# Products of the identity ahead of the first scores, and the first loads in another order

## The chip, the core and the metric

The kernel runs on one core of one Trainium2 chip. The metric is the device time of one execution in microseconds, as the median of several runs. The engines are TensorE (PE in the profile; PEld is its loading of weights), VectorE (DVE), ScalarE (ACT), GpSimd (POOL) and SyncE (SP), whose queue issues all transfers between HBM and the core's memory.

## The reference

Attention over pooled keys and values feeds a gated layer. There are 8 batches, 8 heads, 576 positions, a head size of 64, and eight neighbouring keys (and values) are averaged to one, so that 72 remain:

```python
k_p = k.reshape(B, H, Sp, pool, D).mean(axis=3)
v_p = v.reshape(B, H, Sp, pool, D).mean(axis=3)
scores = scale * np.matmul(q, k_p.transpose(0, 1, 3, 2))
scores = scores - np.max(scores, axis=-1, keepdims=True)
attn = np.exp(scores)
attn = attn / (np.sum(attn, axis=-1, keepdims=True) + 1e-09)
x = np.matmul(attn, v_p)            # 4608 tokens x 512
a, b = x @ w_a, x @ w_b             # 512 x 1536 each
out = (a * b) @ w_out               # 1536 x 512
```

## The kernel before, in words

The 4608 tokens are 36 chunks of 128 tokens for the attention and 9 tiles of 512 tokens for the layer. The inner size 1536 is cut into 12 blocks f. Numbers of the layer are carried as a high and a low part (`xh`, `xl`; `jab` holds both parts of a block of `w_a` and `w_b`, `jo_open` those of `w_out`), and each product is three matmuls. Tiles 0 to 2 run one after the other (`psa`, `psb` are the two gates, `acc` the output); tiles 3 to 8 run in pairs with sums of blocks (`bank_psa`, `bank_psb`, `bank_att`, `pair`).

The opening is what the change touches. The first batch's keys come as four pieces `early_k` (they lie in the tile `wo_first`), each the rows of two heads. DVE sums eight neighbours (`kp`, L909), ACT scales the sums into a block-diagonal tile (`kdiag`, L914 to L916), and for each chunk of 128 queries TensorE makes the scores in two halves of four heads, `psc_..._0` from key pieces 0 and 1 and `psc_..._2` from pieces 2 and 3. DVE takes maxima (`m`), ACT exponentials (`s`), DVE the reciprocals (`z`) and the probabilities (`pr`, and a remainder `rem` for the last eight of the 72 pooled keys). TensorE turns those (`ptr`, `ptr_rem`), ACT copies them out (`early_p`, then `p`), and `po` is the product with the values, from which `xh` and `xl` follow. The first two batches' values and the second batch's keys are pooled by TensorE itself (`pvp` and `pkp`; a `pkp` matmul has only 16 columns). Four chunks (0 to 3) make tile 0; their queries are `early_q` (they lie in `wab_75` in the order of instructions).

Two things are made on the way: the identity `ident` (POOL), which the turning needs, and the weights, whose 64-bit words come over the same queue into `words_ab` and `words_o` and are turned into numbers by ACT and DVE (L528, L535, L251, L247).

The order of all instructions is not written out by hand. Every piece of work is a chain of operations with a rank (a due time), and `Schedule.run` places them one by one, on the engine whose next operation can start first by a table of costs (L175 to L200). Some operations may be placed on one of two engines: `pr` on DVE or POOL, `y` (the output's copy) on ACT or DVE. So an early edit can move operations much later. Each engine runs its own list strictly in that order. `load_early` (L486) is one chain with the highest rank; its transfers stand first in SP's queue. A chunk waits for the mark of its queries, and the loading of weight words for the mark of the last early queries (L506). Only the instructions at L1644 to L1646 are written ahead of the planner.

Of the kernel before, what the change touches and what calls it, by code (L numbers as in the profile page):

```python
# [19 lines left out]
P = 128  # L20
# [18 lines left out]
LAG = 5  # L39
BY_HEAD, LESS_MAX, COPIED = range(3)  # L40
PAIRED_OUT = 1, 2
PAIR_MARGIN, GIVE_MARGIN, SUMS_LATE = 0.0, 6.0, -30.0
XRANK, GIVE_ON, XON = -0.9, 0, ("dve", "pool")
LAGS = [2, 2, 2, 2, 4, 3]
# [36 lines left out]
class Schedule:  # L81
# [27 lines left out]
    def mark(self, *what):  # L109
        self.done.add(what)  # L110
# [93 lines left out]
def attn_moe_kernel(ctx: ExitStack, tc: tile.TileContext, q, k, kn, v, vn, vr, wa, wb, wo, out):  # L204
    nc = tc.nc
# [5 lines left out]
    mark, done = sch.mark, sch.done  # L211
# [10 lines left out]
    def place(pool, shape, dtype, tag, name):  # L222
        t = pool.tile(shape, dtype, tag=tag, name=name, bufs=1)
        sch.alias[t.name] = tag
        return t
# [47 lines left out]
    def dma(out, in_, rank=None):  # L273
        n = 4
        for d in out.shape:
            n *= d
        return Op((SD,), lambda e: nc.sync.dma_start(out, in_), [out], [in_], {SD: EVERY + n * BYTE}, rank)
# [36 lines left out]
    ident = const.tile([P, P], F32, name="ident")  # L314
# [6 lines left out]
    def xslot(x, name, dtype=F32R):  # L321
        return place(sb, [P, NK * NT], dtype, f"x{x}", name)
# [17 lines left out]
    early = sum(t == 0 for t in tile_of)  # L340
# [15 lines left out]
    jo = [xslot(6, "jo_open").rearrange("p (k h c) -> p k h c", k=2, h=2)]  # L356
    streamed = {("o", t1 * NF + f) for p, (_, t1) in enumerate(PAIRS) if p not in PAIRED_OUT for f in range(NF)}
    stream, combos, temps = {}, {}, []
# [6 lines left out]
    def bank(tag, name, dtype=F32):  # L365
        return place(ps, [P, 512], dtype, tag, name)
# [15 lines left out]
    early_q = wab[2][:, :early * 512].rearrange("p (c g s) -> p c g s", c=early, g=NK)  # L382
# [28 lines left out]
    for p, (t0, t1) in enumerate(PAIRS):  # L411
        order += [("both", p, f) for f in range(NF)] + [("rest", p, 0)]
        if p not in PAIRED_OUT:
            order += [("out", t1, f) for f in range(NF)]
    lasting = {"in": 24 * 0.228, "out": 12 * 0.228, "both": 54 * 0.228, "rest": 8 * 0.228}
    due, at = {}, 28.0
    for item in order:
# [3 lines left out]
        at += lasting[item[0]]  # L421
        if item[0] == "both" and item[1] in PAIRED_OUT:
            at += 9 * 0.228
# [4 lines left out]
    stored = {NF + f for f in range(LAG, NF)}  # L428
    apart = [pair for p, pair in enumerate(PAIRS) if p not in PAIRED_OUT]
    stored |= {t1 * NF + f for _, t1 in apart for f in range(NF)}  # L430
    uses, upcoming = [], {name: [] for name in ("ab", "o", "h")}
    for kind, t, f in order:
        if kind == "out":
            uses.append(t * NF + f)
        elif kind == "both" and t not in PAIRED_OUT:
            uses.append(PAIRS[t][0] * NF + f)
# [11 lines left out]
    def chunk_due(i):  # L448
        t = tile_of[i]
        if t < 2:  # L450
            return (-20.0 + 0.01 * i) if t == 0 else JOIN + STEP * (i - early)
        group = next((g for g in PAIRS if t in g), (t,))
        before = tile_due[group[0] - 1]
        share = (i * P + P - group[0] * NT) / (NT * len(group))
        return before + (tile_due[t] - before) * share - 45.0
# [3 lines left out]
    def queries(i):  # L459
        return q[i].rearrange("p (g s) -> p g s", g=NK)  # L460
# [3 lines left out]
    def rows_in(j):  # L464
        return min(P, S - j * P)
# [18 lines left out]
        mark("mask")  # L484

    def load_early():  # L486
        yield dma(early_q[:, 0], queries(0))
        mark("early_q", 0)
        for g in range(NK):
            yield dma(early_k[:, g, :], k[0, :, g, :])  # L490
            mark("early_k", g)
        yield dma(early_q[:, 1], queries(1))
        mark("early_q", 1)
        for j in range(NK + 1):
            rows = rows_in(j)
            yield dma(early_v[j][:rows], vn[0, j * P:j * P + rows])
            raws["v", 0, j] = early_v[j]
        for i in range(2, early):
            yield dma(early_q[:, i], queries(i))
            mark("early_q", i)  # L500

# [3 lines left out]
    def load_words(name):  # L505
        yield W(("early_q", early - 1))  # L506
        for f in range(NF):
            yield W(("converted", name, f - 1))
            for n, x in enumerate(name):
                yield dma(area[name][:, n * 1024:(n + 1) * 1024], w_dram[x][:, f, :].bitcast(I32), lead_of(name, f) - 6.0)  # L510
            mark("words", name, f)
# [144 lines left out]
    def loads():  # L656
# [4 lines left out]
        for p, (t0, t1) in enumerate(PAIRS):  # L661
            if p in PAIRED_OUT:
                for f in range(NF):
# [143 lines left out]
    def need(b):  # L807
        return min(chunk_due(i) for i in of_batch(b))

    def load_raw():  # L810
        yield W(("early_k", NK - 1))
        for kind, src in ("k", kn), ("v", vn):
            for j in range(NK + 1):
                n, rows = j + (NK + 1 if kind == "v" else 0), rows_in(j)
                if n < 8:
                    t = wab[1][:, n * DM:(n + 1) * DM]
                else:
                    kv_of[kind, 1, j] = yield from take(kv)
                    t = place(sb, [P, S], F32, kv_of[kind, 1, j], f"{kind}raw_1_{j}")
                yield dma(t[:rows, :DM], src[1, j * P:j * P + rows], need(1) - (20.0 if kind == "k" else 10.0))  # L820
                raws[kind, 1, j] = t
        for b in range(2, B):
            for kind in "kv":
                for x in range(NK if kind == "k" else NK + NG):
                    at = yield from take(kv)
                    t = place(sb, [P, S], F32, at, f"{kind}raw_{b}_{x}")
                    kv_of[kind, b, x] = at
                    if kind == "k":
                        yield dma(t, k[b, :, x, :], need(b) - 20.0)
                    else:  # L830
                        t = t[:, :D * POOL]
                        if x < NK:
                            yield dma(t, v[b, :, x, :], need(b) - 10.0)
                        else:
                            yield dma(t[:NR], vr[b, :, x - NK, :], need(b) - 10.0)
                    raws[kind, b, x] = t
# [805 lines left out]

    with tc.manual_schedule():
        nc.scalar.copy(rounded, ident)  # L1644
        for t in kdiag[0], unused, *vdiag, kdiag[1]:
            nc.gpsimd.memset(t.bitcast(F32), 0.0)  # L1646
        sch.free[SG], sch.free[SV] = 8.0, 2.0
        sch.spawn(load_early(), -5.0)
        sch.spawn(load_raw(), 0.0)
        sch.spawn(constants(), EIGHTH)  # L1650
        for b in range(B):
            sch.spawn(summed_keys(b) if b == 1 else load_keys(b), need(b) - 14.0 if b > 1 else need(b) - 3.0)
            sch.spawn(
                summed_values(b) if b < 2 else load_values(b),
                need(b) - 4.0 if b > 1 else need(b) - 1.0 if b else VALUES_0,
            )
        for i in range(NCH):
            sch.spawn(chunk(i), chunk_due(i))
        for name in ("ab", "o"):
            sch.spawn(load_words(name), 0.0)  # L1660
            sch.spawn(convert_weights(name), 0.0)
        for kind, t, f in order:
            if kind == "rest":
                continue
            x = (PAIRS[t][0] if kind == "both" else t) * NF + f
            if kind == "out":
                if t < 2:
                    sch.spawn(split_weight("o", x), due[kind, t, f] - 10.0)
                elif t < STD:
                    sch.spawn(load_weight("o", x), due[kind, t, f] - 8.0)  # L1670
                if x in stored:
                    sch.spawn(fetch_gated(x), due[kind, t, f] - 20.0)
            elif kind == "both":
                if t not in PAIRED_OUT:
                    sch.spawn(load_weight("o", x), due[kind, t, f])
            elif x < NF:
                sch.spawn(split_weight("ab", x), due[kind, t, f] - 8.0)
            elif not (t == 1 and f >= LAG):
                sch.spawn(load_weight("ab", x), due[kind, t, f] - 16.0)
        sch.spawn(sums_of_weights(), due["in", 1, NF - 1])  # L1680
        sch.spawn(loads(), 0.0)
        sch.spawn(attention_over(), 0.0)
        sch.spawn(sums_of_pairs(), 0.0)
        sch.spawn(late_places(), 0.0)
        for p in range(len(PAIRS)):
            sch.spawn(sums_of_x(p), due["both", p, 0] - 12.0)
        for t in range(2, STD):
            sch.spawn(whole_x(t), due["in", t, 0] - 15.0)
        sch.spawn(first_outs(), 1e9)
        sch.spawn(first_ins(), 2e9)  # L1690
        sch.spawn(main(), 2e9)
        sch.run()
# [51 lines left out]
```

## Time and profile before

| | |
|---|---|
| median of 3 runs | 978.2 us (976.83 to 978.72) |
| the profiled execution | 977.0 us, its span 975.2 us (the other 1.8 us lie around the span) |
| TensorE busy | 954.6 us, 98% of the span |
| DVE, ACT, POOL busy | 714.4, 414.4, 135.7 us |
| first matmul | 7.72 us after the span's start |
| mean granted clock of TensorE | 0.996 |

The page gives busy time by engine, then the span in slices. The chain that ended last is followed back from the last instruction: it names what the end waited for at every moment. A window's row gives, for a stretch of the span, the busy time of each engine with the number of instructions, then the granted clock of TensorE and the transfers. A row of the timeline is start, duration, engine, line, operation, out<-in, shape and count, and in brackets the idle time before it with what ended it. One fp32 matmul of the program is two records in the trace (the eight score matmuls of the first two chunks are 16 records), a transposition is one.

### The profile page before, as it was taken

Reading aid. Unit: us, or ns where it says so; the run is one execution under the profiler, and the core shown is the slowest. Engines: PE = TensorE matmul, PEld = TensorE weight load, DVE = VectorE, ACT = ScalarE, POOL = GpSimd, SP = SyncE. Lnnn points to the kernel's source line nnn. Section 1 sums busy time; section 2 is a strip of 40 time slices with the busy share of each in tenths; the row PEclk is TensorE's granted clock in tenths of the full one; section 3 lists DMA queues with packets and bytes.
Section 4 is the critical chain, followed back from the end, with each engine's and each line's share of the span. In section 5 each row is a group of like instructions: output and inputs, shape, how many; then the busy total and the mean of one; then the engine's idle time right before and its main releaser. Section 6 shows DMA issues by size and latency. Waiting matters only on the chain.

```text
span 975.2 us, 13044 instructions
## 1 busy us (share of the span) xinstructions
PE 954.6 (98%) x4502; PEld 788.6 (81%) x4502; DVE 714.4 (73%) x1182; ACT 414.4 (42%) x849; POOL 135.7 (14%) x113
## 2 busy tenths in 40 slices
PE   6999999999999999999999999999999999999997
PEld 5778888888888888888888878878888787888885
DVE  6899889899575864789845448156668989676687
ACT  5897656565554553554331124134221422412230
POOL 1001000000000000111212222122212425212221
PEclk9899999999999999999999999999999999999999
DMA  9789899899888999589888899776555756875632
GB/s 311 249 295 316 282 321 319 282 332 327 295 301 288 316 327 294 185 295 312 286 254 272 253 344 341 240 267 215 170 171 173 264 176 197 265 218 169 198 118 87
DMA packets 134978, 251.75 MB, mean 258 GB/s; under 512 B 10688, under 2 KB 46784, under 8 KB 134912
## 3 DMA queue, kind: packets, MB, share of 16 engines
q1 hardware_dynamic: 134912, 250.91, 76.9%
q8 instruction: 36, 0.59, 0.3%
q14 instruction: 30, 0.25, 0.1%
HBM read 191.37 MB, written 59.51 MB: 257 GB/s over the span
## 4 chain that ended last, share of the span: by engine, by line
PE 90%; DVE 4%; DMA 3%; ACT 2%; issue 0%; SPq 0%; POOL 0%; DVEq 0%; ACTq 0%; POOLq 0%
PE acc L303 16%; PE bank_psb L303 13%; PE psa L303 10%; PE psb L303 10%; PE bank_att L303 10%; PE bank_psa L303 9%; PE pair L303 8%; PE psc L303 4%; PE po L303 4%; PE last_acc L303 2%; PE ptr L300 2%; PE last L303 1%; DMA pair_tmp<-od 1%; PE pvp L303 1%; DMA words_ab<-in_wb 1%; DMA j<-jd 1%
## 5 line engine op out<-in xcount | busy, mean ns | idle before, releaser
L303 PE MATMUL bank_psb<-x,j 128*128 128x512 f32 x648 | 166.2, 391 | 1.0 <-DVE x L240 0.4
L303 PEld LDWEIGHTS bank_psb<-x,j 128*128 128x128 f32 x648 | 120.8, 188 | 27.7 <-DVE x L240 0.9
L303 PE MATMUL bank_psa<-x,j 128*128 128x512 f32 x432 | 110.8, 392 | 1.3 <-ACT pr L262 1.3
L303 PE MATMUL bank_att<-x,j 128*128 128x512 f32 x432 | 110.7, 391 | 0.7 <-DVE late_p L240 0.5
L303 PE MATMUL psb<-xh,jab 128*128 128x512 f32 x288 | 101.0, 400 | 0.0
L303 PE MATMUL psa<-xh,jab 128*128 128x512 f32 x288 | 99.3, 397 | 0.6 <-DVE jab L240 0.5
L303 PEld LDWEIGHTS bank_att<-x,j 128*128 128x128 f32 x432 | 80.4, 188 | 18.6 <-DVE late_p L240 0.9
L303 PEld LDWEIGHTS bank_psa<-x,j 128*128 128x128 f32 x432 | 80.4, 188 | 18.5 <-ACT pr L262 1.7
L303 PEld LDWEIGHTS psa<-xh,jab 128*128 128x128 f32 x288 | 53.9, 188 | 12.3 <-DVE jab L240 1.2
L303 PEld LDWEIGHTS psb<-xh,jab 128*128 128x128 f32 x288 | 54.1, 188 | 10.7
L303 PE MATMUL acc<-jo_later,hh 128*128 128x512 f32 x192 | 62.2, 405 | 0.1
L303 PE MATMUL acc<-jo_open,hh 128*128 128x512 f32 x192 | 61.4, 401 | 0.0
L303 PE MATMUL psa<-xl,jab 128*128 128x512 f32 x144 | 56.3, 391 | 0.0
L303 PE MATMUL psb<-xl,jab 128*128 128x512 f32 x144 | 56.2, 390 | 0.0
L240 POOL TENSOR_TENSOR x<-x,x 128x512 fp32r<-128x512 f32 x7 | 11.2, 1611 | 289.3 <-ACT x L262 287.4
L303 PEld LDWEIGHTS psc<-kdiag,q 128*128 128x128 f32 x288 | 42.4, 191 | 5.8 <-issue 1.2
L303 PE MATMUL psc<-kdiag,q 128*128 128x144 f32 x288 | 46.8, 290 | 0.1
L303 PE MATMUL po<-p,vdiag 128*128 128x256 f32 (+3 forms) x184 | 44.4, 345 | 0.5 <-ACT p L262 0.5
L303 PE MATMUL pair<-combos_jo,w 128*128 128x512 f32 x153 | 40.1, 393 | 1.7 <-DVE sums_tmp L240 0.9
L303 PEld LDWEIGHTS acc<-jo_open,hh 128*128 128x128 f32 x192 | 34.5, 188 | 6.1
L303 PEld LDWEIGHTS acc<-jo_later,hh 128*128 128x128 f32 x192 | 33.6, 188 | 5.6 <-ACT hh L262 0.5
L303 PE MATMUL acc<-jo_later,hl 128*128 128x512 f32 x96 | 37.9, 395 | 0.1
(287 smaller groups left out, 1914.3 us busy)
## 6 DMA issues: line engine op xcount, KB each, us to landing
j<-jd SPq DMA_DIRECT2D x108, 512.0 KB, 6.6
jab<-jd SPq DMA_DIRECT2D x34, 512.0 KB, 6.0
jd<-jab SPq DMA_DIRECT2D x24, 512.0 KB, 4.9
jo_later<-od SPq DMA_DIRECT2D x24, 512.0 KB, 5.1
w<-wd SPq DMA_DIRECT2D x44, 256.0 KB, 5.2
j<-jd SPq DMA_DIRECT2D x36, 256.0 KB, 6.9
w<-od SPq DMA_DIRECT2D x33, 256.0 KB, 5.0
q<-in_q SPq DMA_DIRECT2D x32, 256.0 KB, 5.7
```

The costliest lines, as they stand in the source:

```text
L240: run = lambda e: vec[e].tensor_tensor(out=out, in0=in0, in1=in1, op=op)
L300: nc.tensor.transpose(to, lhs, rhs)
L303: nc.tensor.matmul(to, lhs, rhs, start=start, stop=stop, skip_group_check=bool(skip))
```

## The change

First, twenty fp32 products of the 128x128 identity with itself are issued on TensorE ahead of everything that the planner places. They go to the bank `acc0`, which the first scores also use, and nobody reads them. Second, `load_early` loads the first two key pieces ahead of the first queries, and the queries of chunks 1 to 3 ahead of the first batch's values; before, the first queries came first of all, and those of chunks 2 and 3 after the values.

```diff
+QUERIES_AT, BEFORE_V, WARM = 2, 4, 20
...
     def load_early():
-        yield dma(early_q[:, 0], queries(0))
-        mark("early_q", 0)
         for g in range(NK):
+            if g == QUERIES_AT:
+                yield dma(early_q[:, 0], queries(0))
+                mark("early_q", 0)
             yield dma(early_k[:, g, :], k[0, :, g, :])
             mark("early_k", g)
-        yield dma(early_q[:, 1], queries(1))
-        mark("early_q", 1)
+        for i in range(1, BEFORE_V):
+            yield dma(early_q[:, i], queries(i))
+            mark("early_q", i)
         for j in range(NK + 1):
             rows = rows_in(j)
             yield dma(early_v[j][:rows], vn[0, j * P:j * P + rows])
             raws["v", 0, j] = early_v[j]
-        for i in range(2, early):
+        for i in range(BEFORE_V, early):
             yield dma(early_q[:, i], queries(i))
             mark("early_q", i)
...
         nc.scalar.copy(rounded, ident)
+        for n in range(WARM):
+            warm = bank("acc0", "warm") if not n else warm
+            nc.tensor.matmul(warm[:, :P], ident, ident, start=True, stop=True)
```

The head of SP's queue, before (`wab_75` with `in_q` are queries, `wo_first` key pieces, `wo_rest` and `wab_75` with `in_vn` values, `words_ab` weight words):

```order
L277 DMA wab_75<-in_q 128x512
L277 DMA wo_first<-in_k 128x576 x4
L277 DMA wab_75<-in_q 128x512
L277 DMA wo_rest<-in_vn 128x512 x4
L277 DMA wab_75<-in_vn 64x512
L277 DMA wab_75<-in_q 128x512 x2
L277 DMA words_ab<-in_wa 128x1024
L277 DMA words_ab<-in_wb 128x1024
```

and with the change:

```order
L278 DMA wo_first<-in_k 128x576 x2
L278 DMA wab_75<-in_q 128x512
L278 DMA wo_first<-in_k 128x576 x2
L278 DMA wab_75<-in_q 128x512 x3
L278 DMA wo_rest<-in_vn 128x512 x4
L278 DMA wab_75<-in_vn 64x512
L278 DMA words_ab<-in_wa 128x1024
L278 DMA words_ab<-in_wb 128x1024
```

The same thirteen transfers stand ahead of the weight words; the first queries went behind two key pieces, and two loads of queries went ahead of five of values.

The head of TensorE's list, before (`psc` scores, `pvp` pooled values, `ptr` turned probabilities; the last number of a name tells the tile's instance):

```order
L303 MATMUL psc_0_161<-kdiag_77,wab_75 128x144 x2
L303 MATMUL psc_0_167<-kdiag_77,wab_75 128x144 x2
L303 MATMUL psc_2_174<-kdiag_77,wab_75 128x144 x2
L303 MATMUL psc_2_175<-kdiag_77,wab_75 128x144 x2
L303 MATMUL pvp_0_199<-wo_rest,wab_75 128x512 x3
L303 MATMUL psc_0_218<-kdiag_77,wab_75 128x144 x2
L303 MATMUL pvp_0_199<-wo_rest,wab_75 128x512
L303 MATMUL psc_2_222<-kdiag_77,wab_75 128x144 x2
L300 MATMUL ptr_237<-ident,pr_216 128x128 x4
```

and with the change:

```order
L1650 MATMUL warm<-ident 128x128 x20
L304 MATMUL psc_0_180<-kdiag_77,wab_75 128x144 x2
L304 MATMUL psc_0_188<-kdiag_77,wab_75 128x144 x2
L304 MATMUL psc_2_195<-kdiag_77,wab_75 128x144 x2
L304 MATMUL psc_2_196<-kdiag_77,wab_75 128x144 x2
L304 MATMUL psc_0_204<-kdiag_77,wab_75 128x144 x2
L304 MATMUL psc_2_217<-kdiag_77,wab_75 128x144 x2
L304 MATMUL pvp_0_223<-wo_rest,wab_75 128x512 x4
L301 MATMUL ptr_263<-ident,pr_244 128x128 x4
```

The warm products stand in front, and the scores of the third chunk moved ahead of all pooled values.

TensorE's list between the last `po` of the first 256 tokens and the first `po` of the next 256, before (`pkp` the second batch's keys, `ptr_rem` the turned remainder):

```order
L303 MATMUL pkp_226<-eighth,wab_74 128x16 x4
L303 MATMUL pkp_226<-eighth,wab_74 128x8 x4
L300 MATMUL ptr_371<-ident,pr_342 128x128 x4
L300 MATMUL ptr_rem<-rounded,rem_343 96x128 x2
L300 MATMUL ptr_393<-ident,pr_324 128x128 x4
L300 MATMUL ptr_rem<-rounded,rem_325 96x128 x2
L303 MATMUL psc_0_407<-kdiag_77,q_187 128x144 x2
L303 MATMUL po_0_413<-p_1_366,vdiag_79 128x256
```

and with the change:

```order
L304 MATMUL pkp_253<-eighth,wab_74 128x16 x2
L301 MATMUL ptr_371<-ident,pr_338 128x128 x4
L304 MATMUL pkp_253<-eighth,wab_74 128x16 x2
L301 MATMUL ptr_rem<-rounded,rem_339 96x128 x2
L304 MATMUL pkp_253<-eighth,wab_74 128x16
L304 MATMUL pkp_253<-eighth,wab_74 128x8 x4
L301 MATMUL ptr_412<-ident,pr_383 128x128 x4
L301 MATMUL ptr_rem<-rounded,rem_384 96x128 x2
L304 MATMUL po_0_428<-p_1_369,vdiag_79 128x256
```

The third chunk's probabilities are turned between the small `pkp` matmuls instead of after them, and the scores ahead of `po` now follow it. After that the lists differ in many places (TensorE up to row 1425 of some 1920, DVE up to row 714 of 1143), and in which engine takes an operation: with the change POOL has three of the `pr` (before none), one `xl` (before none) and one more low part of the sums `x`, and one less of `jo_open`; DVE has three of the twenty copies `y` that ACT had. From there to the end all lists agree.

## Prediction

> **What bounds the kernel now.** I read the page's busy times first, then the span in stretches of 25 us, then the chain of waits over the first 75 us, and last the granted clock.
>
> ```profile
> PE 954.6 (98%) x4502; PEld 788.6 (81%) x4502; DVE 714.4 (73%) x1182; ACT 414.4 (42%) x849; POOL 135.7 (14%) x113
> 0.00:25.00 25.00, 17.28 (x100) 14.62 (x100) 16.72 (x37) 14.24 (x54) 4.68 (x19) 1.00 0.96 310
> 25.00:50.00 25.00, 24.58 (x121) 19.67 (x121) 22.00 (x38) 21.28 (x50) 0.00 (x0) 0.86 0.75 254
> 50.00:75.00 25.00, 23.45 (x124) 18.86 (x123) 23.51 (x48) 22.88 (x74) 0.00 (x0) 1.00 0.85 294
> 75.00:100.00 25.00, 25.00 (x119) 20.69 (x118) 22.64 (x33) 17.25 (x31) 2.64 (x2) 1.00 0.89 314
> 375.00:400.00 25.00, 25.00 (x126) 20.96 (x126) 14.00 (x28) 10.16 (x22) 0.00 (x0) 1.00 0.86 263
> ```
>
> After the length of each stretch come the busy times of PE, PEld, DVE, ACT and POOL, then the clock. From 75 to 400 us TensorE is busy without a gap, and from 400 us on the change leaves every list as it was. So what TensorE gains in the first 75 us it keeps to the end, if the new order opens no gap between 75 and 400 us; and it can gain nothing there. In the first 75 us there are three losses: 7.7 us before the first matmul, a clock of 0.86 between 25 and 50 us, and 1.55 us of gaps between 50 and 75 us, where ACT and DVE are over 90% busy. The chain shows them one by one:
>
> ```profile
> 1.66 4.50 DMA wo_first<-in_k
> 7.72 4.18 PE psc L303 x16
> 11.90 2.92 PE pvp L303 x6
> 14.82 0.49 PE psc L303 x4
> 15.31 0.86 PE pvp L303 x2
> 16.17 0.49 PE psc L303 x4
> 23.67 1.20 PE po L303 x6
> 24.87 2.15 PE pkp L303 x16
> 27.03 1.06 PE ptr L300 x4
> 28.11 0.85 ACT p L262 x2
> 30.02 1.08 PE psc L303 x4
> 31.10 3.36 PE po L303 x12
> 39.85 1.39 PE psa L303 x6
> 65.47 0.94 ACT jab L262
> 66.44 1.24 DVE jab L240
> ```
>
> Sixteen score records take 4.18 us at first, 0.26 each, and four take 0.49 us at 14.82, 0.12 each: TensorE starts slow and is at full rate about 4.6 us after its first matmul, although the records grant it 1.00 there. The weight loads date the change:
>
> ```profile
> 7.69 3.86 PEld L303 LDWEIGHTS psc<-kdiag,wab 128*128 128x128 f32 x16 [7.69 <-issue]
> 11.46 0.58 PEld L303 LDWEIGHTS pvp<-wo_rest,wab 128*128 128x128 f32 x2
> 12.52 0.19 PEld L303 LDWEIGHTS pvp<-wo_rest,wab 128*128 128x128 f32 x1 [0.48 <-issue]
> 12.95 0.19 PEld L303 LDWEIGHTS pvp<-wo_rest,wab 128*128 128x128 f32 x1 [0.24 <-issue]
> 26.00:26.50 0.50, 0.50 (x5) 0.50 (x5) 0.50 (x3) 0.50 (x3) 0.00 (x0) 0.62 0.41 143
> 32.50:33.00 0.50, 0.50 (x4) 0.41 (x2) 0.50 (x1) 0.07 (x1) 0.00 (x0) 0.55 1.01 418
> ```
>
> From 12.52 us on a load for `pvp` follows every 0.43 us; from 11.46 to 12.52 there are two, at 0.53. The rise lies near 12.3 us, 4.6 us after the first matmul. Later the clock falls again. A mean of 0.62 in the half microsecond from 26.0 and of 0.55 in that from 32.5 puts the slow stretch at 26.12 to 32.95, 6.83 us. It follows the long run of `pkp` (16 columns) and `ptr`, with no dense matmul between the `po` that ends at 24.87 and the scores at 30.02.
>
> [...]
>
> **The start, step by step.** The warm products need only `ident`:
>
> ```profile
> 1.49 0.30 POOL masks.py:199 TENSOR_SCALAR_AFFINE_SELECT ident<-ident 128x128 f32<-128x128 f32 x1
> 8.47 0.66 ACT L915 ACTIVATE kdiag<-kp 64x144 f32<-64x144 f32 x2 [0.84 <-DVE kp L255]
> 16.66 0.44 PE ptr L300 x4
> ```
>
> They start at about 1.85 us. Twenty are 40 records. A record costs 0.24 us slow (3.86 over 16; the slow `ptr`, also 128 columns, took 1.06 over 4, so 0.27) and 0.12 at full rate (0.49 over 4; `ptr` at full rate 0.44 over 4, so 0.11). If the rise comes 4.6 us after the start again, 19 records are slow and 21 fast: 1.85 + 4.6 + 2.5 = 9.0 us. The bounds of the rise are 3.4 and 6.8 us (half and all of the slow stretch), which gives 8.4 and 10.1 us. The first scores stand behind the products on TensorE's queue. Their keys and queries cannot need longer than before (7.72), so the warm products delay them by 0.7 to 2.4 us against before: the earlier keys are hidden completely behind them. Being issued first, those pieces only make sure that `kdiag` waits ready.
>
> From 9.0 us all runs at full rate: six groups of scores (three chunks) at 0.49 and four pairs of `pvp` at 0.86 are 2.94 + 3.44 = 6.4 us, so 15.4 us. The second half of the scores needs the fourth key piece, which is still the fifth transfer of the queue; its `kdiag` stands at 8.47 + 0.66 = 9.1, before the first two groups are through (10.0). Before, the same work ended at 16.17 + 0.49 = 16.66 us. TensorE leads by **1.3 us** (bounds 0.2 and 1.9, from 10.1 and 8.4 us).
>
> **The transfers.** Two loads of queries pass five of values.
>
> ```profile
> 3.55 1.86 SPq L277 DMA_DIRECT2D wo_rest<-in_vn  x4
> 6.18 0.57 SPq L277 DMA_DIRECT2D wab<-in_vn  x1
> 6.93 1.07 SPq L277 DMA_DIRECT2D wab<-in_q  x2
> wab<-in_vn SPq DMA_DIRECT2D x1, 128.0 KB, 6.3
> 14.66 0.65 PE L303 MATMUL psc<-kdiag,wab 128*128 128x144 f32 x4
> ```
>
> At 310 GB/s (the first stretch's rate), 512 KB are 1.7 us. The last values, issued at 6.18 before (6.3 us to landing, 12.5), land by about 14; the last `pvp` of the run of four wants the fourth piece at 11.9 + 3 x 0.86 = 14.5, the fifth piece only later. Cost nothing, hidden behind the scores of three chunks; without them it would be about 1 us. The third chunk's queries, which before landed near 13 and were used at 14.66, are now there when the second chunk's scores end. Weight words stand where they stood: no change.
>
> **The light stretch.** The lead of 1.3 us reaches the `pkp` and `ptr` work. With the change that work is interleaved, but there is still no dense matmul from the `po` of the first 256 tokens (before, end 24.87) to the next, and that one waits for ACT:
>
> ```profile
> 26.12:32.95 6.83, 6.41 (x27) 5.36 (x26) 5.98 (x12) 5.46 (x13) 0.00 (x0) 0.50 0.45 154
> 16.00:26.00 10.00, 10.00 (x81) 9.43 (x79) 8.02 (x23) 8.70 (x32) 0.00 (x0) 1.00 1.04 320
> 60.00:68.00 8.00, 6.45 (x35) 4.65 (x34) 7.37 (x15) 7.87 (x27) 0.00 (x0) 1.00 0.87 277
> ```
>
> So I expect the clock to fall again for about as long. Whatever of the lead lies within the slow stretch is worth half. Of the 6.83 us before, the chain lies 1.9 us (28.11 to 30.02) nearly all with ACT and DVE; the other 4.9 us are TensorE's work at half rate, so 2.5 us were lost. [...]
>
> **From 40 to 75 us** ACT is busy 7.87 of 8 us: the chain goes through ACT `jab` and DVE `jab`, which feed the next gates. ACT and DVE have the same work as before, so they pass the lead on: 0.9, and the gaps of 1.55 us stay (bounds: gone, or double).
>
> **From 75 to 400 us** the order is new, with three `pr` and one `xl` on POOL.
>
> ```profile
> L240 POOL TENSOR_TENSOR x<-x,x 128x512 fp32r<-128x512 f32 x7 | 11.2, 1611 | 289.3 <-ACT x L262 287.4
> L240 DVE TENSOR_TENSOR pr<-s,z 128x512 f32<-128x512 f32 x20 | 13.8, 690 | 0.6
> ```
>
> An operation of this size takes 1.61 us on POOL and 0.69 on DVE, 0.92 more, four times 3.7 us. They are hidden behind the gates' matmuls (1.4 us for six), as everything was there before; I take nothing, with 0 and 3.7 as bounds.
>
> **Sum.** 1.3 - 0.4 = 0.9 us faster. Against the profiled execution that is 977.0 - 0.9 = 976.1; it was 1.2 under the median, so the forecast against the median is 978.2 - 0.9 = **977.3 us**. Since a measurement of this kernel tells about 0.2% (2.0 us) from no change, this reads as the same.
>
> **Rivals.**
>
> *The clock does not fall.* The `pkp` run is now cut by `ptr` and `ptr_rem`. If that counts as activity, 2.5 us come back: 978.2 - 1.3 - 2.5 = 974.4. For it: before, the clock stayed 1.00 from 16 to 26 us in a mixture of scores, `pkp`, `ptr` and `po`. Against it: scores and `po` are missing from the new stretch. Chance 0.15.
>
> [...]
>
> *The lead is eaten.* [...] The same. Chance 0.17.
>
> *The opening gaps go.* With everything earlier, the 1.55 us between 60 and 68 us vanish too: 978.2 - 0.9 - 1.55 = 975.8. Against it: ACT is full there. Chance 0.05.
>
> *Slower: a POOL `pr` holds TensorE.* Where DVE has a turn to spare, a `pr` on POOL ends 0.92 us later, and `ptr` stands in TensorE's fixed list between dense matmuls, so a late `pr` stops all of them. From more than the margin that the planner left (over 2.9 us in all) it decides: four on the path are 978.2 - 0.9 + 3.7 = 981.0. Against it: between 75 and 400 us nothing waited before. Chance 0.13.
>
> The forecast itself (lead of 0.3 to 1.9, so 976.3 to 977.9) has 0.50. Faster: 0.15 + 0.05 and 0.10 of the forecast's upper end, 0.30; slower 0.13; the same 0.57. The range that leaves out two in ten is 974.8 to 980.0.
>
> **What would show it.** Right: `warm` of 40 records from 1.9 to about 9.0 us; the following `psc` at 0.12 us a record; `ptr` of the first chunk near 15.4; a granted clock of 0.50 again between about 25 and 33 us; TensorE busy 25.00 in each stretch from 75 to 400 us. Wrong: no stretch at 0.50 (a gain near 3.8 us), or a first `psc` after 10 us, or a gap that names `pr` on POOL as its releaser.

## The result and the profile after

The changed kernel takes 983.15 us (median of six runs, 982.59 to 987.2) against 976.63 us for the kernel before measured beside it (974.74 to 978.72). The ratio, which is that of the means, is 1.0077 with a 95% interval of 1.0061 to 1.0093: **slower by 7.5 us between the means and 6.5 us between the medians**, where 0.9 us faster was forecast, and outside the range. Three executions that lie far above all others, two of the kernel before (near 1946 us) and one of a kernel of the experiments (1372 us), are left out of every median and ratio here. The profiled execution took 982.64 us, its span is 980.9 us, 5.7 more than the 975.2 of before.

The opening went better than forecast. TensorE's rows of the timeline of the changed kernel, in its first 16 us (start, duration, engine, line, operation, shape and count):

```profile
1.84 6.40 PE L1650 MATMUL warm<-ident 128*128 128x128 f32 x40 [1.84 <-POOL ident masks.py:199]
8.35 3.18 PE L304 MATMUL psc<-kdiag,wab 128*128 128x144 f32 x24
11.36 3.60 PE L304 MATMUL pvp<-wo_rest,wab 128*128 128x512 f32 x8
14.79 0.60 PE L301 MATMUL ptr<-ident,pr 128*128 128x128 f32 x4
```

The first `ptr` stands at 14.79 (forecast 15.4; before, in the same view, 16.50). The first gate product `psa` starts at 34.58 us, before at 39.59; 0.5 us of that is a group of scores that stood ahead of it before and now follows.

Then TensorE loses more than it won. The stretches of 25 us in which the changed kernel's TensorE is idle (length, then busy time of PE, PEld, DVE, ACT, POOL, clock, transfers):

```profile
0.00:25.00 25.00, 23.06 (x155) 20.41 (x155) 18.21 (x43) 17.19 (x60) 4.67 (x19) 1.00 0.96 315
25.00:50.00 25.00, 23.50 (x117) 17.86 (x117) 21.42 (x35) 20.81 (x48) 0.00 (x0) 1.00 0.85 294
50.00:75.00 25.00, 20.96 (x106) 17.22 (x105) 21.72 (x45) 19.87 (x68) 0.00 (x0) 0.93 0.79 270
200.00:225.00 25.00, 24.19 (x118) 20.00 (x117) 21.77 (x39) 15.13 (x27) 1.29 (x1) 1.00 0.93 313
375.00:400.00 25.00, 24.24 (x127) 20.14 (x125) 14.60 (x26) 10.54 (x24) 0.00 (x0) 1.00 0.80 262
400.00:425.00 25.00, 23.17 (x132) 19.68 (x132) 20.45 (x38) 16.09 (x34) 2.70 (x2) 1.00 0.46 149
550.00:575.00 25.00, 23.69 (x105) 19.29 (x104) 9.71 (x15) 4.89 (x9) 5.14 (x4) 1.00 0.92 286
```

and those of before that the prediction did not show:

```profile
200.00:225.00 25.00, 25.00 (x123) 20.95 (x122) 23.06 (x42) 15.21 (x29) 0.00 (x0) 1.00 0.94 334
400.00:425.00 25.00, 24.86 (x133) 20.73 (x132) 20.04 (x37) 15.52 (x33) 4.38 (x3) 1.00 0.66 220
550.00:575.00 25.00, 24.82 (x110) 20.20 (x109) 8.30 (x12) 3.59 (x6) 5.18 (x4) 1.00 0.92 313
```

More idle than before, stretch by stretch: 1.1 (25 to 50), 2.5 (50 to 75), 0.8 (200 to 225), 0.8 (375 to 400), 1.7 (400 to 425) and 1.1 us (550 to 575), together 8.0. In the first 25 us idle time and warm products come to 0.6 more than the idle time of before. Against these 8.6 us stands work done in less time: TensorE is busy 958.1 us, of which 6.4 are the warm products, so 951.7 for all the rest, 2.9 less than the 954.6 of before (at the start the 24 score records take 3.18 us, 0.13 each, and the clock is 1.00 instead of 0.86 between 25 and 50 us). 8.6 - 2.9 = 5.7 us, the difference of the spans.

The waits of TensorE in the changed kernel (who waited, for whom: us in all, times, longest):

```profile
PE psc L304 <- ACT p L263: 2.3, 2, 1.7
PE warm L1650 <- POOL ident masks.py:199: 1.8, 1, 1.8
PE acc L304 <- DVE hl L241: 1.8, 1, 1.8
...
PE acc L304 <- ACT s L271: 1.7, 1, 1.7
PE bank_att L304 <- ACT temp L263: 1.3, 1, 1.3
PE psc L304 <- ACT s L263: 1.3, 2, 0.8
```

From 40 to 80 us, the kernel before has only these:

```profile
PE psa L303 <- DVE jab L240: 0.5, 1, 0.5
PE po L303 <- ACT p L262: 0.5, 1, 0.5
PE ptr_rem L300 <- ACT s L270: 0.5, 1, 0.5
```

No row of the change names POOL, apart from the start, where the products wait for `ident`. What such a wait is, ACT and then TensorE show at 52 to 55 us:

```profile
52.06 1.04 ACT L263 CAST jab<-wab 128x1024 fp32r<-128x1024 f32 x1 [1.88 <-DVE wab L241]
53.01 0.61 ACT L263 CAST hh<-h 128x512 fp32r<-128x512 f32 x1
53.53 0.58 ACT L263 COPY p<-ptr 128x512 f32<-128x512 f32 x1
...
51.91 0.60 PE L301 MATMUL ptr<-ident,pr 128*128 128x128 f32 x4
54.16 0.76 PE L304 MATMUL psc<-kdiag,q 128*128 128x144 f32 x4 [1.65 <-ACT p L263]
```

The turned probabilities `ptr` were there at 52.5, and the next scores need the bank that their copy `p` frees. But ACT's list has two casts ahead of the copy, the first of which waited for DVE until 52.06 itself. So the copy came at 53.53, and TensorE, whose list is as fixed, stood for 1.65 us. At 65 us four exponentials hold a bank that `acc` wants (1.67 us). In the stretch from 550 us a copy of `bank_att` comes late on ACT behind two casts (1.3 us). There ACT's order is that of before, and it is DVE that makes the sums for the casts later than before (the first cast waits 1.47 us for them).

This is one execution of the changed kernel. Three more traces of the same lists are in the next section (the changed kernel again, the loads alone, and the lists without either edit). Five rows of the list of waits stand in all four: `psc` behind `p`, `acc` behind `s`, `acc` behind `hl`, `bank_att` behind `temp` and `po` behind `p`. Together they are 8.1 to 8.5 us, where the two traces of the kernel before have 2.1 and 2.9 us of waits in all between 10 and 600 us. The idle time from 200 to 225 and from 375 to 400 us does not recur so: the other three traces have 0.4, 0 and 0 us there.

### The profile page after: what moved, and what is told of

Same layout as the page of the kernel before. It is cut to its first block, busy times and chain, and to the rows that moved or that the text cites. A ratio compares the mean times of both kernels' runs of the same rounds, so it can differ in the third digit from the quotient of the medians.

```text
span 980.9 us, 13141 instructions
## 1 busy us (share of the span) xinstructions
PE 958.1 (98%) x4542; PEld 791.8 (81%) x4542; DVE 715.6 (73%) x1181; ACT 413.7 (42%) x846; POOL 140.1 (14%) x117
## 5 line engine op out<-in xcount | busy, mean ns | idle before, releaser
L304 PE MATMUL pair<-combos_x,w 128*128 128x512 f32 x144 | 37.0, 390 | 0.7 <-DVE sums_tmp L241 0.7
```

The lines of the kernel that those rows point to most:

```text
L304: nc.tensor.matmul(to, lhs, rhs, start=start, stop=stop, skip_group_check=bool(skip))
```

## Experiments

The change does two things at once. Its edits (products, loads) act on the chip directly. And since the planner gets other loads, it makes other lists for every engine. The rivals were: the loads or the products themselves cost; the re-made list costs, whatever the edits do; and, for the second group, whether it is this list in particular (because the planner knows nothing of the products, or of how the new loads land) or any list that is made anew, that of before being a good draw. The letters D (a draw) and S (something special to this change) in the expectations of that group mean these two. Ratios are to the kernel before measured beside each kernel; for the three groups measured together it took 975.87, 976.08 and 975.94 us.

**The products alone.** The kernel before with the twenty products; the lists and loads are those of before.

```diff
         nc.scalar.copy(rounded, ident)
+        for n in range(20):
+            warm = bank("acc0", "warm") if not n else warm
+            nc.tensor.matmul(warm[:, :P], ident, ident, start=True, stop=True)
```

> The twenty products alone; transfers and every engine's list as before. Theory L (the list that the planner made anew costs the time): no slower than before; the first scores start near 8.4 us as in the changed kernel but at full rate, so 974 to 976.5 us, and TensorE has no gap between 75 and 400 us. Rival W (the products cost the time, by holding TensorE's queue or by what they do to its clock later): 980 to 983 us.

Measured: 976.77 us, ratio 1.0006 (0.9993 to 1.0019), just above the range of theory L and far from that of W. The products neither cost nor bring anything that can be told from nothing. One gap stands between 75 and 400 us against the expectation, 1.3 us for a load of queries; the second trace of the kernel before has it too (0.8 us).

**The loads alone**, with the lists that the planner makes of them.

```diff
-QUERIES_AT, BEFORE_V, WARM = 2, 4, 20
+QUERIES_AT, BEFORE_V, WARM = 2, 4, 0
```

> The two edits of the loads alone, with the list that the planner makes of them (that of the change, without the products). Theory L: 983 to 986 us, with the gaps of the changed kernel between 200 and 225, 375 and 425 and 550 and 575 us. Rival W: 976 to 977 us.

Measured: 983.76 us, 1.0085 (1.0063 to 1.0108). The whole loss is here, without a single warm product. Of the expected gaps those from 400 to 425 (1.8 us) and from 550 to 575 us (1.4) are there, those from 200 to 225 and from 375 to 400 us are not.

**Both edits on the chip, the lists of before.** The planner is shown the loads of before, and each of the thirteen transfers that it places issues the one that the change has at that place. TensorE, DVE, ACT and POOL keep their lists of before word for word.

```diff
+        for planned, real in zip(early_loads(0, 2), early_loads(2, 4)):
+            op = dma(*early_load(*planned))
+            op.run = lambda e, real=real: nc.sync.dma_start(*early_load(*real))
+            yield op
```

> Both edits carried out on the chip (twenty products, transfers in the new order), but the planner is told the old order of loads, so that PE, DVE, ACT and POOL keep the list of before word for word, and SP's differs only in its first thirteen transfers. Theory L: 973 to 976 us, faster than before. Rival T (the order of transfers costs the time, values coming late): 980 to 983 us.

Measured: 976.15 us, 1.0004 (0.9993 to 1.0016): no loss, but not the gain that theory L expected either.

**Neither edit on the chip, the lists of the change.** The same the other way round: no products, transfers in the order of before, the planner shown the new one.

```diff
+        for planned, real in zip(early_loads(2, 4), early_loads(0, 2)):
```

> The opposite: no products, the thirteen transfers in the old order, but the planner is told the new order, so that PE, DVE, ACT and POOL have the list of the change. Theory L: 982 to 986 us, the loss of the change without its edits. Rivals W and T: 976 to 978 us.

Measured: 984.06 us, 1.0095 (1.0064 to 1.0126). The waits from 10 to 600 us are those of the change:

```profile
PE psc L303 <- ACT p L262: 2.3, 2, 1.7
PE acc L303 <- DVE hl L240: 1.8, 1, 1.8
PE acc L303 <- ACT s L270: 1.7, 1, 1.7
PE bank_att L303 <- ACT temp L262: 1.4, 1, 1.4
```

These two runs settle the main question. The edits without the list cost nothing that can be measured, the list without the edits costs everything.

**Other lists, made without either edit.** In the planner's table the time that a transfer takes to land is raised by 10 ns, and in a second kernel the fixed part of a transfer's time by 1 ns.

```diff
-BYTE, EVERY, LAND, AHEAD = 1 / 330e3, 0.1, 1.8, 1.5
+BYTE, EVERY, LAND, AHEAD = 1 / 330e3, 0.1, 1.81, 1.5
...
+BYTE, EVERY, LAND, AHEAD = 1 / 330e3, 0.101, 1.8, 1.5
```

> Neither edit. The planner's table alone is touched: it believes that a transfer lands after 1.81 instead of 1.80 us. That has no meaning on the chip, but the lists differ from TensorE's row 30 on, in about as many places as those of the change. Theory S (the list of the change is slow because of what it was told, queries ahead of values): 975 to 977 us, as before. Theory D (any list that is made anew is a draw, and the list of before is a good one): anywhere from 976 to 986 us, slower than before in most cases, with gaps of TensorE at other places than in the changed kernel.

Measured: 987.61 us, 1.0126 (1.0103 to 1.015), slower than even theory D allowed.

> Neither edit. The planner believes that each transfer costs 0.101 instead of 0.100 us beside its bytes. Theory S: 975 to 977 us. Theory D: another draw, 976 to 986 us, not the time of the run with 1.81 us.

Measured: 981.53 us, 1.0061 (1.0046 to 1.0076). Of the 4210 rows of TensorE's list at least 515 would have to be moved to make the order of before into that of the change, 503 and 554 for these two. Their waits, of the first and then the second, from 10 to 600 us:

```profile
PE bank_att L303 <- ACT temp L262: 2.7, 1, 2.7
PE po L303 <- ACT p L262: 1.2, 1, 1.2
PE psa L303 <- DVE jab L240: 1.0, 1, 1.0
PE psc L303 <- ACT p L262: 0.9, 1, 0.9
```

```profile
PE bank_att L303 <- ACT temp L262: 1.4, 1, 1.4
PE po L303 <- ACT p L262: 1.2, 1, 1.2
PE psa L303 <- DVE jab L240: 1.0, 1, 1.0
PE psc L303 <- ACT p L262: 0.9, 1, 0.9
```

The kind is the same (TensorE behind a copy or a cast on ACT or DVE), mostly at other tiles. Theory S, which expected no loss from either, is out. A change of 10 ns in a table, with no work altered, costs at least as much as the whole change under study, and one of 1 ns nearly as much.

**The planner told of the products.** The products, the loads of before, and TensorE taken until 9.0 us in the planner's book.

```diff
         sch.free[SG], sch.free[SV] = 8.0, 2.0
+        sch.free[SPE] = 9.0
```

> The twenty products, transfers in the old order, and the planner is told that TensorE is taken until 9.0 us (in the change it knows nothing of the products). Theory S: 975 to 977 us, since the list now fits the chip better. Theory D: a third draw, 976 to 986 us; that the planner was told the truth does not help.

Measured: 982.9 us, 1.0067 (1.0047 to 1.0087). A truer plan of the opening did not give a better list.

**Products and keys first, queries as before** (the lists of TensorE, DVE, ACT and POOL stay those of before; only the change's third constant, which puts queries 2 and 3 ahead of the values, makes them anew).

```diff
-QUERIES_AT, BEFORE_V, WARM = 2, 4, 20
+QUERIES_AT, BEFORE_V, WARM = 2, 2, 20
```

> The change without its last part: twenty products and the first queries behind two key pieces, but queries 2 and 3 stay behind the values. All lists but the first six transfers are then those of before, so both theories expect no loss: 974 to 977 us. If the key pieces in front do harm, 979 us or more.

Measured: 976.37 us, 1.001 (0.9997 to 1.0022).

**The opening's order by hand.** Both edits with the lists of before, and the first four `pvp` behind the third chunk's scores, as the change has them at its head. Operations 4, 5, 6 and 8 of TensorE are emitted after operation 9:

```diff
+HOLD = {('pe', 4): 9, ('pe', 5): 9, ('pe', 6): 9, ('pe', 8): 9}
...
+            if (engine, n) in HOLD:
+                self.held.append((engine, HOLD[engine, n], op))
+            else:
+                op.run(engine)
```

> Both edits on the chip, the planner kept on the loads of before, and one more thing by hand: on TensorE the first four products of the values (pvp) are emitted behind the scores of the third chunk, as the changed list has them at its opening. All other rows of every engine stand as before. If the re-made list after the opening is what costs, and not the order that the edit was meant to give, the time is that of the list kept: ratio to before 0.997 to 1.002 (about 976 us). If the values standing behind the scores of three chunks is itself the loss (values late, a later vdiag, a later first po), the ratio is 1.005 or more (above 981 us) and TensorE waits for vdiag or vrem between 15 and 30 us.

Measured: 977.16 us, 1.0009 (0.9994 to 1.0024). The order of the opening that the change was written for costs nothing and brings nothing. Where the lead of these openings goes, the waits of this kernel show:

```profile
PE ptr_rem L315 <- DVE rem L255: 1.4, 1, 1.4
PE bank_psa L318 <- ACT temp L277: 1.1, 1, 1.1
```

1.4 us go where TensorE, being early, waits for the remainder on DVE; the kernel before waits 0.4 to 0.5 us there, so 1.0 us of the lead is lost. The same row, with 1.4, stands in the kernels with products alone, with both edits on the old lists and with keys first. Another 0.7 to 1.1 us go in the stretch from 400 us, at a wait (`bank_psa` behind `temp`) that neither trace of before has.

**One place of the changed list mended.** Two operations of ACT, the copy of `ptr_rem` and an unpacking, go behind four exponentials instead of ahead of them.

```diff
+HOLD = {('act', 108): 113, ('act', 109): 113}
```

> The changed kernel with one place of ACT's list mended by hand: the copy of ptr_rem into p and the unpacking ahead of it, which stand ahead of four exponentials at 62.9 us, are emitted behind them. Nothing else moves. If the wait of 1.67 us of acc at 65 us is owed to that order on ACT, it falls to between 0.4 and 1.0 us and TensorE keeps the lead as far as the next wait; the whole time falls by 0.7 to 1.3 us against the changed kernel of the same call if nothing behind it takes it back, by less than 0.3 us if a later wait does. If the wait is owed to something else (a late score, the clock), it stays above 1.4 us.

> The changed kernel once more, unaltered, as the pair for the kernel with the mended place. If its list is what loses, its waits are those of its first profile (psc behind ACT p 2.3 us in two, acc behind DVE hl 1.8, acc behind ACT s 1.7) and the ratio to before is 1.006 to 1.009. If the lost time were a draw of the execution, the waits fall at other places or with other names and the ratio lies below 1.004.

Measured: 981.09 us, 1.0056 (1.0034 to 1.0078), against 986.43 us, 1.0107 (1.0086 to 1.0129), for the changed kernel measured beside it, which missed its expected ratio on the high side. The waits of the changed kernel are again the same ones (2.4, 1.8 and 1.7 us at the same tiles). At the mended place, TensorE in the changed kernel's first trace, then in the mended one:

```profile
65.12 0.74 PE L304 MATMUL acc<-jo_open,hh 128*128 128x512 f32 x2 [1.67 <-ACT s L271]
...
67.09 0.99 PE L304 MATMUL po<-p,vdiag 128*128 128x192 f32 x2
```

```profile
64.81 0.74 PE L319 MATMUL acc<-jo_open,hh 128*128 128x512 f32 x2 [1.33 <-ACT s L286]
...
66.74 0.57 PE L319 MATMUL po<-p,vdiag 128*128 128x192 f32 x2
```

The wait fell to 1.33, less than expected, because the exponentials now wait themselves for the maxima:

```profile
63.44 0.32 ACT L286 ACTIVATE s<-psc,m 128x72 f32<-128x72 f32 x1 [0.35 <-DVE m L271]
```

So ACT's order accounts for 0.34 us of it. The rest was expected to go too and did not: the maxima come no earlier from DVE, whose list was left as it is. That the whole time fell by 5.3 us against the pair is more than this place can give, and the clock can account for all of it. The missing share of the granted clock, times the span, estimates what half-rate stretches cost at most. By that it is 1.5 us an execution in the mended kernel (mean clock 0.9985) and 6.7 us in its pair (0.993). Without it the means are 979.9 and 979.5 us, so the mended place brought no gain that can be seen. The kernel before, measured beside them, has 3.6 us of it and 972.3 without, so the clock is not what makes the changed list slow. How the loss is divided among the places of the list stays open.

**The kernel before, once more**, for a second trace.

> The kernel before once more, for a second trace. If the half-rate stretch near 26 to 33 us is a draw of the execution, it is missing here or lies elsewhere, and the span is then 972 to 975 us; if it is owed to the work, it stands at 26 to 33 us again and the span is 975 to 976 us.

Measured: 976.52 us, span 974.7. Its half-rate stretch lies from about 27.6 to 31.0 us and is 3.4 us long, half as long as in the first trace. So its length is a draw. A stretch of that kind near that place was in both, so neither of the two expectations holds as it stands.

## Why the prediction was wrong, step by step

**The start: right in kind, the size too small.** Forecast: 40 records from 1.85 to 9.0 us, and a lead of 1.3 us at the third chunk's scores and values. Measured: 1.84 to 8.24 (6.40 us, 0.16 a record) and 1.7 us (the first `ptr` at 14.79 against 16.50), within its bounds. The rise came earlier than the 4.6 us that were taken from before: by the prediction's two prices of a record, about 3.2 us after the start (an estimate). In the trace of the kernel whose planner is told of the products the same 40 records take 7.18 us, in that with the opening by hand 7.39, so this too varies by execution.

**The transfers at nothing: right.** Keys first, alone or with the queries moved too, on the lists of before: 1.001 and 1.0004.

**The light stretch: the rival mostly happened.** The forecast was another stretch at half rate (a granted clock of 0.50). Of five traces with the changed list (one of them with the mended place) four have no half rate from 20 to 50 us, which was the condition of the rival "the clock does not fall"; one has 6.8 us of it. Of six traces with the lists of before (one with four rows moved by hand), five have such a stretch. This suggests that the interleaved order keeps the clock up, but the traces are too few to show it. The rival's gain, a time of 974.4 us, did not come: what was won here was lost behind it. No run shows the 0.4 us that the sum takes off the lead here; the first trace of the change has a clock of 1.00 from 25 to 50 us, the second 0.50 from 26.8 to 33.6 us.

**"ACT and DVE have the same work as before, so they pass the lead on: 0.9, and the gaps of 1.55 us stay": this step failed first, and it is the main one.** The work is almost the same, its order is not. The gaps from 50 to 75 us grew from 1.55 to 4.04 us, above the upper bound of double, and are 4.4 to 5.3 us in the other three traces of these lists. At 52 us the wait is decided by which operation stands first on ACT, not by how much work ACT has. In the lists of before that a products-only kernel keeps, the gaps did stay (23.41 us busy from 50 to 75, against 23.45).

**"The order is new ... I take nothing", from 75 to 400 us: held within its bounds.** In the first trace TensorE is idle there 1.7 us more (0.8 from 200 and 0.8 from 375 us, the rest near 150), in the other three traces of the same lists 0.4, 0 and 0. The kernel before has 0 in one trace and 0.8 in the other, so no loss from the list is shown here.

**"From 400 us on the change leaves every list as it was": a misreading.** The lists do agree from some row on, but that row is reached later than 400 us. TensorE's last 1944 rows of 4210 agree; before, the last differing products of `bank_att` (the first 90 of 432) end by 520 us. DVE agrees in its last 439 of 1181 rows, which begin near 545 us before and near 551 with the change. The 1.7 us from 400 and 1.1 us from 550 us, 2.8 of the 8.6 us, come of operations ahead of these rows, and both recur in all four traces. A row's number was taken for a time without looking it up in the trace.

**The rival on the slower side: right sign, wrong mechanism.** It put the price on POOL's slower `pr` (0.92 us each). No wait of TensorE between 10 and 600 us names POOL; the releasers are ACT's copies, casts and exponentials, and DVE's `hl`. A chance of 0.13 for slower was too small because the operations that went to a slower engine were priced, and those that merely moved not at all: some 515 rows of TensorE's 4210 and 270 of ACT's 808 stand elsewhere.

**Even without the new list the gain would not have come.** The edits on the lists of before gave 1.0004 (0.9993 to 1.0016), where a gain of 0.9 us would have been 0.9991, just below that interval. A lead of 1.0 us is seen to go in one wait for DVE, and 0.7 to 1.1 us near 400 us. The sum passed the lead of the opening on to the end, and this is the second place where it does not hold.

No version beat both kernels. The edits kept on the old lists are as fast as before, and so the best that these runs offer is the kernel before.

## What to carry to other kernels

Where a planner writes the lists, an edit to its inputs is two edits: the one that was meant, and a new order of hundreds of operations, whose price here was 0.6 to 1.3% in every one of four re-made lists. Separate them by showing the planner the old input while the chip gets the new one (or the reverse) before believing anything about the edit itself. All four were slower, so the list of before was a good draw; how it was come by is not on record. When such a list is made anew, expect a loss, and look up in the trace at what time its last differing row runs.

## What the runs showed of the hardware

The half-rate stretches of TensorE (a granted clock of 0.50) differ between executions of the same lists. Between 20 and 38 us the two traces of before have 6.8 and 3.4 us of it, and three of the four with warm products on the same lists (one of them with four rows moved by hand) 3.4 us, the fourth none. With the changed list four traces have none and one has 6.8. The other three re-made lists have 3.4, 3.4 and 17 us. Up to 550 us such a stretch is 3.4, 6.8, 10.2 (the loads alone, from 65.2 us) or about 17 us long (the planner told of the products, to 37.7 us). The second trace of the change has three: 6.8 us from 26.8, 3.4 us from 71.1 and 3.4 us from 422.7 us.

Some of the stretches come behind waits, some do not. Below are the 3.41 us ahead of a fall and the 3.41 us behind it, at half rate, in the changed kernel's first trace, then in the second trace of before:

```profile
63.41:66.82 3.41, 1.74 (x12) 1.56 (x12) 2.68 (x8) 3.41 (x18) 0.00 (x0) 1.00 0.92 347
66.82:70.23 3.41, 3.41 (x13) 2.93 (x12) 2.09 (x6) 2.33 (x8) 0.00 (x0) 0.50 0.61 224
```

```profile
24.20:27.61 3.41, 3.41 (x27) 3.26 (x27) 3.08 (x10) 3.33 (x11) 0.00 (x0) 1.00 0.55 186
27.61:31.03 3.42, 2.92 (x15) 2.51 (x16) 3.38 (x7) 2.92 (x9) 0.00 (x0) 0.50 0.05 7
```

TensorE was busy 1.74 of the 3.41 us ahead of the one fall and all of those ahead of the other, there by its list mostly with `pkp` of 16 and 8 columns and transpositions.

A wait of the same length is followed by a fall in one execution and by none in another. The wait of `acc` for `hl` near 420 us is 1.8 us long in all five traces with the changed list. In three the clock fell to 0.50 within 1.0 us of its end (the lists of the change without its edits, the second trace of the change, the mended kernel), in the changed kernel's first trace and with the loads alone it stayed at 1.00. First a trace of the lists without the edits, then the first of the changed kernel:

```profile
418.80 0.67 PE L303 MATMUL acc<-jo_later,hl 128*128 128x512 f32 x1 [1.82 <-DVE hl L240]
415.55:418.97 3.42, 1.60 (x9) 1.08 (x8) 3.42 (x4) 2.58 (x7) 1.78 (x2) 1.00 0.40 153
418.97:422.38 3.41, 3.41 (x12) 2.94 (x13) 3.41 (x7) 1.63 (x2) 0.00 (x0) 0.50 0.43 154
```

```profile
419.11 0.50 PE L304 MATMUL acc<-jo_later,hl 128*128 128x512 f32 x1 [1.83 <-DVE hl L241]
414.98:418.39 3.41, 2.30 (x12) 1.63 (x10) 3.41 (x4) 3.37 (x9) 2.55 (x2) 1.00 0.42 153
418.39:421.80 3.41, 2.69 (x15) 2.40 (x16) 3.41 (x6) 2.12 (x4) 0.12 (x1) 1.00 0.27 91
```

In the changed kernel's first trace the 3.41 us up to the end of the wait (415.70 to 419.11) hold 1.58 us of TensorE's work, hardly other than the 1.60 ahead of the fall in the other. What decides between the two is not shown. At a clock of 0.50 such a stretch of 3.41 us does at most what takes 1.7 us at 1.00, so a fall costs up to a further 1.7 us of the work behind the wait (an estimate from the length and the clock). That fits the spread of the changed kernel: its four runs near 983 us have mean clocks of 0.996 to 0.998, the two at 986.1 and 987.2 us 0.995 and 0.992. Those two runs have no trace, so for them the link is argued, not shown.
